# Second layer of an attention and two-layer expert kernel: how the seven Strassen products of a step are added up

## The chip, the cores and the metric

One core of a Trainium2 chip runs the whole kernel in one launch. The metric is device time in microseconds (us). Five engines work side by side, each through its own list of instructions in order: TensorE (PE; its weight loads have rows of their own, PEld), VectorE (DVE), ScalarE (ACT), GpSimd (POOL) and SyncE (SP), which here issues the DMAs. Matmul results land in PSUM, eight banks of 128 x 512 fp32; all else lives in SBUF.

## The reference, cut to what matters

Windowed attention gives a 2304 x 512 matrix x; a gated layer (512 to 1536 to 512) follows; then the second layer, which the change is about: eight experts, each a 512 to 1024 to 512 network with a ReLU, weighted by a router's probabilities.

```python
def _moe2_ref(x, w_gate, w1, w2):            # x (2304, 512), w1 (8, 512, 1024), w2 (8, 1024, 512)
    ...                                       # P: softmax of x @ w_gate, balanced 8 times by rows and columns
    out = np.zeros((N, D), dtype=np.float32)
    for e in range(E):
        h = np.maximum(x @ w1[e], 0.0)
        ye = h @ w2[e]
        out += P[:, e:e + 1] * ye
    return out.astype(np.float32)
```

## The kernel before, in words

**Precision.** Each fp32 operand is held as a high part rounded to fp32r and a low part (the rest). A product of two operands is three matmuls: high x high, high x low, low x high. `split` (L541 to L543) makes the parts: ACT casts the high one (L542), DVE subtracts to get the low one (L543).

**Steps.** The second layer runs over 96 steps (g, e, j): 3 groups of 768 tokens, 8 experts, 4 column pairs of w1. A step takes two 128-column blocks of w1 (j and j + 4) and computes hidden values for both, for both 384-token halves of the group. These four 128 x 384 results are one 2 x 2 block product, done with seven products in the Strassen-Winograd form, named M1 to M7. Each product is six matmuls of 128 x 384 (`emit_m`, L765, matmul L772): three passes by two halves of the depth. Passes one and two read the high weights, pass three the low ones, so the high weights of a product are last read by its 4th matmul. Products alternate between PSUM banks 6 and 7 (L767) in the order of `ORDER` (L763): M1, M6, M2, M7, M4, M5, M3.

**Adding up, before.** Each product is read out alone. ACT copies M1 (L785). DVE adds M6 to it (L787, u2), M2 to M1 (L789, the first result), M7 to u2 (L792, u3), subtracts M4 from u3 (L794, the third result), adds M5 to u3 (L797, the fourth result) and to u2 (L798), and M3 to u2 (L801, the second result). Each finished result goes through ReLU: ACT writes the high part (L805), DVE the low part (L806). A product's first weight load waits until the last reader of its bank's former content is done.

**Second matrix.** `emit_l2` (L810, matmul L818) multiplies the hidden values of the step before with w2: 36 matmuls of 128 x 512 into banks 0 to 5. In the program a step is its seven products, then the L818 matmuls of the step before, so the hidden values have a step's time to get ready. After four steps DVE adds each bank, weighted by P, to the output (L833).

**Weights.** The Strassen sums of w1 (`split_w1`, L604) are made on DVE (L610 once, then L609 three times, 128 x 256 each) in one scratch buffer, `o_sum`, and split into `o_wc[j]`. Four casts (and four L543) serve a step: A11 with A12 (used by M1 and M2), A22 (M4), S1 with S2 (M5 and M6), S3 with S4 (M7 and M3). They are written into the buffer that the running step still reads, so each cast waits for the 4th matmul of the last product that reads that piece, and the next sums wait until the scratch is read. w2 is split into `o_w2`. Both come by 256 KB DMAs (L501) into a ring of six slots; a DMA is issued when the slot's former content has been split. The x operands are split once per group (`split_x`, L621).

**Order.** The list `ev` gives the program's order, but the framework's scheduler sets the order on each engine; once set, an engine runs its list strictly in order. The router's column sums (`emit_cols`, L741) use eight columns of bank 7 and are put between products by `hooks` (L1013 to L1015).

Of the kernel before, what the change touches and what calls it, by code (L numbers as in the profile page):

```python
# [12 lines left out]
ALU = mybir.AluOpType  # L13
# [4 lines left out]
def attention_moe_moe2(  # L18
# [13 lines left out]
    nc = tc.nc  # L32
# [23 lines left out]
    HT = 128 * HTT  # L56
# [3 lines left out]
    for grp in groups:  # L60
        for half in grp:
            toks = [b * S + s + i for b, s, n in half for i in range(n)]
            for i in range(HTT):
                c = toks[i * 128:(i + 1) * 128]
# [89 lines left out]
    def area(name):  # L154
        if name not in areas:
            areas[name] = pool.tile([128, sizes[name]], F32R if name[-1] == "R" else F32, tag=name[0], name="area_" + name)
        return areas[name]

    PS = [psum.tile([128, 512], F32, name=f"ps{i}") for i in range(8)]

    def sl(o, n, r=False, p=slice(0, 128)):
        a = area(o.area)[p, o.off:o.off + n]
        if o.area[-1] == "R":
            return a if r else a.bitcast(F32)
        assert not r
        return a
# [319 lines left out]
    def load_w():  # L486
        n = w_load[0]
        if n >= len(raw_keys):
            return
        w_load[0] += 1  # L490
        key, i = raw_keys[n]
        src = sources(key)[i]
        if wide(key):
            dst = sl(o_wide[n % NWIDE], 1024).bitcast(I32)
        elif key[0] == "x":
            dst = sl(o_raw[n % NRAW], HT)
        else:
            dst = sl(o_raw[n % NRAW], 512)
        if len(src.shape) == 3:
            dst = dst.rearrange("p (k f) -> p k f", k=src.shape[1])  # L500
        nc.sync.dma_start(out=dst, in_=src)  # L501
# [39 lines left out]
    def split(src, hi, hi_f, lo):  # L541
        nc.scalar.copy(hi, src)  # L542
        nc.vector.tensor_tensor(out=lo, in0=src, in1=hi_f, op=ALU.subtract)  # L543

    def raw_slots(key):
        cnt = sum(1 for r in raw_keys if r[0] == key)
        n = w_next[0]
        assert raw_keys[n][0] == key
        w_next[0] += cnt
        return [o_raw[(n + i) % NRAW] for i in range(cnt)]  # L550
# [70 lines left out]
    def split_x(key):  # L621
        kk = key[2]
        b11, b12, b21, b22 = (sl(o, HT) for o in raw_slots(key))
        t = sl(o_sum, 4 * HT)
        t1, t2, t3, t4 = (t[:, HT * i:HT * i + HT] for i in range(4))
        sub = lambda o, a, b: nc.vector.tensor_tensor(out=o, in0=a, in1=b, op=ALU.subtract)
        sub(t1, b12, b11)
        sub(t2, b22, t1)
        sub(t3, b22, b12)
        sub(t4, t2, b21)  # L630
        view = lambda r: sl(o_xc, 28 * HT, r).rearrange("p (h m k n) -> p h m k n", h=2, m=7, n=HT)
        xr, xf = view(True), view(False)
        for src, m in ((b11, 0), (t2, 4), (b21, 1), (t3, 5), (t1, 3), (t4, 6), (b22, 2)):
            split(src, xr[:, 0, m, kk, :], xf[:, 0, m, kk, :], xr[:, 1, m, kk, :])
        for _ in range(4):
            load_w()
# [123 lines left out]

    steps = [(g, e, j) for g in range(NS) for e in range(NE) for j in range(NF2 // 2)]

    ORDER = (1, 6, 2, 7, 4, 5, 3)  # L763

    def emit_m(s, m):  # L765
        g, e, j = steps[s]
        ps = PS[6 + (7 * s + ORDER.index(m)) % 2][:, 0:HT]  # L767
        o = o_wc[j]
        i = 0
        for wp, xp in ((0, 0), (0, 1), (1, 0)):  # L770
            for kk in range(2):
                nc.tensor.matmul(  # L772
                    ps,
                    lhsT=sl(o + wp * (WC // 2) + A_OF[m] * 256 + kk * 128, 128, True),
                    rhs=sl(o_xc + xp * 14 * HT + (B_OF[m] * 2 + kk) * HT, HT, True),
                    start=(i == 0),
                    stop=(i == 5),
                )
                i += 1
        t = o_tmp[s % 2]  # L780
        m1, u2, u3, c21 = (sl(t + i * HT, HT) for i in range(4))
        h = o_h[s % 2]
        c = None
        if m == 1:
            nc.scalar.copy(m1, ps)  # L785
        elif m == 6:
            nc.vector.tensor_tensor(out=u2, in0=m1, in1=ps, op=ALU.add)  # L787
        elif m == 2:
            nc.vector.tensor_tensor(out=m1, in0=m1, in1=ps, op=ALU.add)  # L789
            c, i = m1, 0  # L790
        elif m == 7:
            nc.vector.tensor_tensor(out=u3, in0=u2, in1=ps, op=ALU.add)  # L792
        elif m == 4:
            nc.vector.tensor_tensor(out=c21, in0=u3, in1=ps, op=ALU.subtract)  # L794
            c, i = c21, 2
        elif m == 5:
            nc.vector.tensor_tensor(out=u3, in0=u3, in1=ps, op=ALU.add)  # L797
            nc.vector.tensor_tensor(out=u2, in0=u2, in1=ps, op=ALU.add)  # L798
            c, i = u3, 3
        else:  # L800
            nc.vector.tensor_tensor(out=u2, in0=u2, in1=ps, op=ALU.add)  # L801
            c, i = u2, 1
        if c is not None:
            hi, lo = h[2 * i], h[2 * i + 1]
            nc.scalar.activation(sl(hi, HT, True), c, AF.Relu)  # L805
            nc.vector.scalar_tensor_tensor(  # L806
                out=sl(lo, HT, True), in0=c, scalar=0.0, in1=sl(hi, HT), op0=ALU.max, op1=ALU.subtract
            )
# [71 lines left out]
    first = min(att)  # L880
# [130 lines left out]

    late = [("w1", 0, 0, 2), ("w2", 0, 0, 6), ("w1", 0, 0, 3), ("w2", 0, 0, 7)]
    hooks = {1: [("lg", NB - 1, 5)], 3: [("lgt", NB - 1, 5), ("gmax1",)], 5: [("gmax2", 5)]}  # L1013
    for it in range(8):
        hooks[13 + 2 * it] = [("cols", it, 7)]  # L1015
    pos = 0
    add("o", *prev)
    n_steps = len(steps)
# [1 line left out]
    for s in range(n_steps + 1):  # L1020
        for i, m in enumerate(ORDER):
            if s < n_steps:
# [43 lines left out]
    def banks(x):  # L1066
# [39 lines left out]
        "gmax2": lambda bk: emit_gmax2(banks(bk)),  # L1106
        "cols": lambda it, bk: emit_cols(it, banks(bk)),
        "m": emit_m,
        "l2": emit_l2,
    }  # L1110
# [32 lines left out]
```

## Time and profile before

| | |
|---|---|
| time, three runs | 2051.5, 2055.56, 2055.93 us (median 2055.56) |
| the profiled execution | span 2053.0 us from first to last instruction, between the fastest and the median run; the profile gives no other time for it |
| PE busy | 2040.6 us (99%) |
| PEld busy | 1803.5 us (88%) |
| DVE busy | 1473.4 us (72%) |
| ACT busy | 904.1 us (44%) |
| second layer, L772 and L818 | from 550.7 us to the end |

Busy time says how long an engine had an instruction in it. Where PE is busy all the time, what other engines do matters only if PE has to wait for it, and such a wait shows as idle time of PEld with the engine that ended it.

### The profile page before, as it was taken

Reading aid. Unit: us, or ns where it says so; the run is one execution under the profiler, and the core shown is the slowest. Engines: PE = TensorE matmul, PEld = TensorE weight load, DVE = VectorE, ACT = ScalarE, POOL = GpSimd, SP = SyncE. Lnnn points to the kernel's source line nnn. Section 1 sums busy time; section 2 is a strip of 40 time slices with the busy share of each in tenths; the row PEclk is TensorE's granted clock in tenths of the full one; section 3 lists DMA queues with packets and bytes.
Section 4 is the critical chain, followed back from the end, with each engine's and each line's share of the span. In section 5 each row is a group of like instructions: output and inputs, shape, how many; then the busy total and the mean of one; then the engine's idle time right before and its main releaser. Section 6 shows DMA issues by size and latency. Waiting matters only on the chain.

```text
span 2053.0 us, 30730 instructions
## 1 busy us (share of the span) xinstructions
PE 2040.6 (99%) x11189; PEld 1803.5 (88%) x11189; DVE 1473.4 (72%) x2987; ACT 904.1 (44%) x1800; POOL 42.5 (2%) x77
## 2 busy tenths in 40 slices
PE   8999999999999999999999999999999999999999
PEld 6887888888989899899989999989989999999997
DVE  7985555556897777767787677777688777677763
ACT  7756555655634334333343333333444333333331
POOL 3100000000000000000000000000000000000000
PEclk9999999999999999999999999999999999999999
DMA  9984453335622222222242222212224222222200
GB/s 250 271 265 119 109 139 103 109 91 165 186 78 72 62 72 73 62 64 76 63 128 72 73 62 72 72 62 65 75 63 128 75 70 62 72 72 62 69 25 31
DMA packets 235736, 197.05 MB, mean 96 GB/s; under 512 B 66880, under 2 KB 182080, under 8 KB 235584
## 3 DMA queue, kind: packets, MB, share of 16 engines
q1 hardware_dynamic: 235584, 195.10, 33.0%
q8 instruction: 87, 1.43, 0.3%
q14 instruction: 65, 0.53, 0.1%
HBM read 176.18 MB, written 18.87 MB: 95 GB/s over the span
## 4 chain that ended last, share of the span: by engine, by line
PE 96%; DVE 2%; ACT 1%; DMA 0%; issue 0%; DVEq 0%; ACTq 0%
PE ps L818 38%; PE ps L772 34%; PE ps L651 13%; PE ps L669 7%; PE ps L434 1%; PE ps L417 1%; PE ps L297 1%; PE ps L274 0%; DVE area_F L522 0%; DVE area_F L529 0%; PE ps L360 0%; PE ps L689 0%; ACT area_aF L515 0%; DVE area_bF L400 0%; DMA area_F<-saved 0%
## 5 line engine op out<-in xcount | busy, mean ns | idle before, releaser
L818 PE MATMUL ps<-area_aR,area_R 128*128 128x512 f32 x3456 | 808.1, 390 | 0.0
L818 PEld LDWEIGHTS ps<-area_aR,area_R 128*128 128x128 f32 x3456 | 646.7, 188 | 129.4
L772 PE MATMUL ps<-area_bR,area_R 128*128 128x384 f32 x4032 | 725.1, 336 | 0.0
L772 PEld LDWEIGHTS ps<-area_bR,area_R 128*128 128x128 f32 x4032 | 706.1, 188 | 11.3 <-DVE area_F L787 0.8
L542 ACT CAST area_R<-area_F 128x512 fp32r<-128x512 f32 (+1 forms) x528 | 302.2, 578 | 303.7 <-PE ps L772 168.2
L543 DVE TENSOR_TENSOR area_R<-area_F,area_R 128x512 fp32r<-128x512 f32 (+1 forms) x528 | 329.0, 638 | 89.9 <-ACT area_R L542 51.2
L542 ACT CAST area_aR<-area_F 128x512 fp32r<-128x512 f32 x192 | 119.3, 621 | 484.0 <-PE ps L818 470.1
L651 PE MATMUL ps<-area_R 128*128 128x512 f32 (+1 forms) x1440 | 313.6, 372 | 4.7 <-ACT area_F L656 3.3
L543 DVE TENSOR_TENSOR area_aR<-area_F,area_aR 128x512 fp32r<-128x512 f32 x192 | 131.6, 690 | 239.5 <-ACT area_aR L542 239.5
L651 PEld LDWEIGHTS ps<-area_R 128*128 128x128 f32 x1440 | 251.9, 190 | 54.5 <-ACT area_F L656 3.9
L805 ACT ACTIVATE area_R<-area_F 128x384 fp32r<-128x384 f32 x384 | 202.2, 527 | 191.8 <-DVE area_F L801 79.8
L806 DVE SCALAR_TENSOR_TENSOR area_R<-area_F,area_R 128x384 fp32r<-128x384 f32 x384 | 212.1, 552 | 2.0 <-ACT area_R L805 2.0
L669 PE MATMUL ps<-area_R 128*128 128x512 f32 (+1 forms) x720 | 162.6, 374 | 0.3 <-ACT area_R L660 0.3
L669 PEld LDWEIGHTS ps<-area_R 128*128 128x128 f32 x720 | 123.6, 189 | 24.2 <-issue 1.5
L609 DVE TENSOR_TENSOR area_F<-area_F 128x256 f32<-128x256 f32 x288 | 113.7, 421 | 2.4 <-DMA area_F<-in_moe_w_dram 0.3
L787 DVE TENSOR_TENSOR area_F<-area_F,ps 128x384 f32<-128x384 f32 x96 | 53.1, 553 | 73.4 <-PE ps L772 73.4
L833 DVE SCALAR_TENSOR_TENSOR area_F<-ps,area_F 128x512 f32<-128x512 f32 x126 | 94.3, 748 | 13.1 <-PE ps L818 12.6
L658 DVE TENSOR_TENSOR area_F<-area_F,ps 128x512 f32<-128x512 f32 (+1 forms) x60 | 37.9, 632 | 58.4 <-PE ps L651 50.1
L789 DVE TENSOR_TENSOR area_F<-area_F,ps 128x384 f32<-128x384 f32 x96 | 53.2, 554 | 35.6 <-PE ps L772 35.3
L785 ACT COPY area_F<-ps 128x384 f32<-128x384 f32 x96 | 46.0, 479 | 57.7 <-PE ps L772 57.2
L797 DVE TENSOR_TENSOR area_F<-area_F,ps 128x384 f32<-128x384 f32 x96 | 53.1, 553 | 14.4 <-PE ps L772 3.0
L792 DVE TENSOR_TENSOR area_F<-area_F,ps 128x384 f32<-128x384 f32 x96 | 52.7, 549 | 2.9 <-PE ps L772 2.9
(106 smaller groups left out, 1012.2 us busy)
## 6 DMA issues: line engine op xcount, KB each, us to landing
area_F<-in_moe_w_dram SPq DMA_DIRECT2D x384, 256.0 KB, 3.0
area_F<-saved SPq DMA_DIRECT2D x144, 256.0 KB, 2.8
saved<-area_F SPq DMA_DIRECT2D x18, 512.0 KB, 6.8
area_aF<-in_moe_w_gate_dram SPq DMA_DIRECT2D x12, 512.0 KB, 5.9
area_aF<-in_moe_w_val_dram SPq DMA_DIRECT2D x12, 512.0 KB, 6.2
area_aF<-in_moe_w_out_dram SPq DMA_DIRECT2D x12, 512.0 KB, 6.3
area_F<-x2d SPq DMA_DIRECT2D x24, 192.0 KB, 2.4
area_bF<-in_k_dram SPq DMA_DIRECT2D x16, 256.0 KB, 4.9
```

Source lines behind the costliest of these rows:

```text
L542: nc.scalar.copy(hi, src)
L543: nc.vector.tensor_tensor(out=lo, in0=src, in1=hi_f, op=ALU.subtract)
L609: sub = lambda o, a, b: nc.vector.tensor_tensor(out=o, in0=a, in1=b, op=ALU.subtract)
L651: nc.tensor.matmul(ps, lhsT=w3[:, kk, :], rhs=x3[:, kk, :], start=(i == 0), stop=(i == 3 * KD - 1))
L669: nc.tensor.matmul(PS[m][:, 0:n], lhsT=sl(o + 512 * wp + m * 128, 128, True), rhs=sl(oh + 512 * xp, n, True), start=(f == 0 and i == 0), s ...
L772: nc.tensor.matmul(ps, lhsT=sl(o + wp * (WC // 2) + A_OF[m] * 256 + kk * 128, 128, True), rhs=sl(o_xc + xp * 14 * HT + (B_OF[m] * 2 + kk) ...
L787: nc.vector.tensor_tensor(out=u2, in0=m1, in1=ps, op=ALU.add)
L789: nc.vector.tensor_tensor(out=m1, in0=m1, in1=ps, op=ALU.add)
L805: nc.scalar.activation(sl(hi, HT, True), c, AF.Relu)
L806: nc.vector.scalar_tensor_tensor(out=sl(lo, HT, True), in0=c, scalar=0.0, in1=sl(hi, HT), op0=ALU.max, op1=ALU.subtract)
L818: nc.tensor.matmul(PS[i], lhsT=sl(h[2 * q_ + hp] + c0, 128, True), rhs=sl(o + 512 * wp, 512, True), start=(j == 0 and fi == 0 and n == 0), ...
L833: nc.vector.scalar_tensor_tensor(out=a, in0=PS[i], scalar=p, in1=a, op0=ALU.mult, op1=ALU.add)
```

## The change

In the second layer TensorE adds up products itself. One chain runs in bank 6: M1, then M6, M7 and M4 each accumulate on what stands there; a second chain runs in bank 7: M5, then M3. M2 uses bank 7 alone, before M5. Between the products of a chain an engine reads the partial sum. The order is M1, M2, M6, M5, M7, M3, M4. The x operand of M4 changes its sign (L630), so that M4 can be added. ACT now copies three partial sums (M1, M1+M6, M5), DVE does three additions (r1 += M2, r3 += M1+M6+M7, r2 += M5+M3), and the third result is read by the ReLU directly from bank 6. The router's column sums move to places where no chain is open in bank 7.

```diff
-        sub(t4, t2, b21)
+        sub(t4, b21, t2)
...
-    ORDER = (1, 6, 2, 7, 4, 5, 3)
+    ORDER = (1, 2, 6, 5, 7, 3, 4)
+    CHAIN_A, CHAIN_B = (1, 6, 7, 4), (5, 3)
...
-        ps = PS[6 + (7 * s + ORDER.index(m)) % 2][:, 0:HT]
+        ps = PS[6 if m in CHAIN_A else 7][:, 0:HT]
+        first = m in (1, 2, 5)
+        last = m in (4, 2, 3)
...
-                    start=(i == 0),
+                    start=(first and i == 0),
                     stop=(i == 5),
+                    skip_group_check=not first,
...
+        add_ = lambda o: nc.vector.tensor_tensor(out=o, in0=o, in1=ps, op=ALU.add)
         if m == 1:
-            nc.scalar.copy(m1, ps)
+            nc.scalar.copy(r1, ps)
         elif m == 6:
-            nc.vector.tensor_tensor(out=u2, in0=m1, in1=ps, op=ALU.add)
+            nc.scalar.copy(r2, ps)
+        elif m == 5:
+            nc.scalar.copy(r3, ps)
         elif m == 2:
-            nc.vector.tensor_tensor(out=m1, in0=m1, in1=ps, op=ALU.add)
-            c, i = m1, 0
+            add_(r1)
+            c, q_ = r1, 0
         elif m == 7:
-            nc.vector.tensor_tensor(out=u3, in0=u2, in1=ps, op=ALU.add)
-        elif m == 4:
-            nc.vector.tensor_tensor(out=c21, in0=u3, in1=ps, op=ALU.subtract)
-            c, i = c21, 2
-        elif m == 5:
-            nc.vector.tensor_tensor(out=u3, in0=u3, in1=ps, op=ALU.add)
-            nc.vector.tensor_tensor(out=u2, in0=u2, in1=ps, op=ALU.add)
-            c, i = u3, 3
+            add_(r3)
+            c, q_ = r3, 3
+        elif m == 3:
+            add_(r2)
+            c, q_ = r2, 1
         else:
-            nc.vector.tensor_tensor(out=u2, in0=u2, in1=ps, op=ALU.add)
-            c, i = u2, 1
+            c, q_ = ps, 2
...
-    for it in range(8):
-        hooks[13 + 2 * it] = [("cols", it, 7)]
+    for it, at_ in enumerate((12, 14, 16, 19, 21, 23, 26, 28)):
+        hooks[at_] = [("cols", it, 7)]
```

In the changed file the line numbers shift: the matmul of a product is L775, the DVE addition L787, the ACT copies L789 (M1), L791 (M1+M6) and L793 (M5), the ReLU L807 and L808. In the rows below ps_71 is bank 6 and ps_72 bank 7.

On DVE, one step in the middle of the second layer, before (L787 reads M6, L789 M2, L792 M7, L794 M4, L797 and L798 M5, L801 M3):

```order
L787 TENSOR_TENSOR area_F<-area_F,ps_71 128x384
L789 TENSOR_TENSOR area_F<-area_F,ps_72 128x384
L543 TENSOR_TENSOR area_R<-area_F,area_R 128x512
L792 TENSOR_TENSOR area_F<-area_F,ps_71 128x384
L806 SCALAR_TENSOR_TENSOR area_R<-area_F,area_R 128x384
L794 TENSOR_TENSOR area_F<-area_F,ps_72 128x384
L543 TENSOR_TENSOR area_R<-area_F,area_R 128x256
L797 TENSOR_TENSOR area_F<-area_F,ps_71 128x384
L806 SCALAR_TENSOR_TENSOR area_R<-area_F,area_R 128x384
L798 TENSOR_TENSOR area_F<-area_F,ps_71 128x384
L806 SCALAR_TENSOR_TENSOR area_R<-area_F,area_R 128x384
L801 TENSOR_TENSOR area_F<-area_F,ps_72 128x384
```

The same stretch now (the three L787 read M2, then M1+M6+M7, then M5+M3):

```order
L787 TENSOR_TENSOR area_F<-area_F,ps_72 128x384
L543 TENSOR_TENSOR area_R<-area_F,area_R 128x512
L808 SCALAR_TENSOR_TENSOR area_R<-area_F,area_R 128x384
L543 TENSOR_TENSOR area_R<-area_F,area_R 128x512
L610 TENSOR_TENSOR area_F<-area_F 128x256
L787 TENSOR_TENSOR area_F<-area_F,ps_71 128x384
L609 TENSOR_TENSOR area_F<-area_F 128x256
L787 TENSOR_TENSOR area_F<-area_F,ps_72 128x384
L543 TENSOR_TENSOR area_R<-area_F,area_R 128x512
L808 SCALAR_TENSOR_TENSOR area_R<-area_F,area_R 128x384 x2
L808 SCALAR_TENSOR_TENSOR area_R<-ps_71,area_R 128x384
L543 TENSOR_TENSOR area_R<-area_F,area_R 128x256
```

The weight sums of the next w1 block (L610, L609), which stood behind all the additions, have moved in between them; the second L543 (the low part of S1 and S2) and L610 stand right ahead of the addition that reads bank 6 after M7. These three stand so in 81 of the 96 steps.

On ACT, the same step before (L785 copies M1, L805 is the ReLU, L542 the casts: A11 with A12, then A22, then S1 with S2, then S3 with S4):

```order
L785 COPY area_F<-ps_72 128x384
L542 CAST area_R<-area_F 128x512
L805 ACTIVATE area_R<-area_F 128x384
L542 CAST area_R<-area_F 128x256
L805 ACTIVATE area_R<-area_F 128x384
L542 CAST area_R<-area_F 128x512
L805 ACTIVATE area_R<-area_F 128x384
L542 CAST area_R<-area_F 128x512
L805 ACTIVATE area_R<-area_F 128x384
```

And now:

```order
L789 COPY area_F<-ps_71 128x384
L542 CAST area_R<-area_F 128x512
L807 ACTIVATE area_R<-area_F 128x384
L791 COPY area_F<-ps_71 128x384
L542 CAST area_R<-area_F 128x512
L793 COPY area_F<-ps_72 128x384
L542 CAST area_R<-area_F 128x512
L807 ACTIVATE area_R<-area_F 128x384
L542 CAST area_R<-area_F 128x256
L807 ACTIVATE area_R<-area_F 128x384
L807 ACTIVATE area_R<-ps_71 128x384
```

The second cast (S1 with S2) now stands between the copies of M1+M6 and of M5. TensorE's order keeps its shape: in all but the first steps and those around the two group changes it is 42 product matmuls by sixes on alternating banks, then 36 of the second matrix.

## Rows read from the trace of the kernel before

**Rows 1.** The page's head and its busy times by engine.
```profile
span 2053.0 us, 30730 instructions
PE 2040.6 (99%) x11189; PEld 1803.5 (88%) x11189; DVE 1473.4 (72%) x2987; ACT 904.1 (44%) x1800; POOL 42.5 (2%) x77
```
**Rows 2.** The chain that ended last, by engine.
```profile
PE 96%; DVE 2%; ACT 1%; DMA 0%; issue 0%; DVEq 0%; ACTq 0%
```
**Rows 3.** Groups by line: names, shapes, count, then busy us, mean ns, then idle before.
```profile
L772 PEld LDWEIGHTS ps<-area_bR,area_R 128*128 128x128 f32 x4032 | 706.1, 188 | 11.3 <-DVE area_F L787 0.8 <-ACT area_F L785 0.5 <-ACT area_R L542 0.4
...
L787 DVE TENSOR_TENSOR area_F<-area_F,ps 128x384 f32<-128x384 f32 x96 | 53.1, 553 | 73.4 <-PE ps L772 73.4
```
**Rows 4.** Timeline of PE over one step: start us, duration us, engine, line, count.
```profile
1201.24 7.49 PE L772 MATMUL ps<-area_bR,area_R 128*128 128x384 f32 x42
1208.58 8.36 PE L818 MATMUL ps<-area_aR,area_R 128*128 128x512 f32 x36
1216.78 0.51 PE L772 MATMUL ps<-area_bR,area_R 128*128 128x384 f32 x2
```
**Rows 5.** Timeline of all engines in the same step, ACT and DVE rows.
```profile
1201.42 1.37 DVE L543 TENSOR_TENSOR area_aR<-area_F,area_aR 128x512 fp32r<-128x512 f32 x2 [3.65 <-ACT area_aR L542]
1202.56 0.48 ACT L785 COPY area_F<-ps 128x384 f32<-128x384 f32 x1 [0.50 <-PE ps L772]
1203.62 0.55 DVE L787 TENSOR_TENSOR area_F<-area_F,ps 128x384 f32<-128x384 f32 x1 [0.83 <-PE ps L772]
1204.24 0.62 ACT L542 CAST area_R<-area_F 128x512 fp32r<-128x512 f32 x1 [1.20 <-PE ps L772]
1204.59 0.56 DVE L789 TENSOR_TENSOR area_F<-area_F,ps 128x384 f32<-128x384 f32 x1 [0.42 <-PE ps L772]
1205.06 0.69 DVE L543 TENSOR_TENSOR area_R<-area_F,area_R 128x512 fp32r<-128x512 f32 x1
1205.18 0.53 ACT L805 ACTIVATE area_R<-area_F 128x384 fp32r<-128x384 f32 x1 [0.32 <-DVE area_F L789]
1205.66 0.55 DVE L792 TENSOR_TENSOR area_F<-area_F,ps 128x384 f32<-128x384 f32 x1
...
1211.74 0.42 DVE L610 TENSOR_TENSOR area_F<-area_F 128x256 f32<-128x256 f32 x1
```
**Rows 6.** Timelines of single instructions, short windows in that step.
```profile
1200.76 0.62 ACT L542 CAST area_aR<-area_F 128x512 fp32r<-128x512 f32 x1 [5.52 <-PE ps L818]
1203.87 0.51 PE L772 MATMUL ps<-area_bR,area_R 128*128 128x384 f32 x2
1204.22 0.19 PEld L772 LDWEIGHTS ps<-area_bR,area_R 128*128 128x128 f32 x1
1212.08 0.76 DVE L609 TENSOR_TENSOR area_F<-area_F 128x256 f32<-128x256 f32 x2
1212.87 0.42 DVE L609 TENSOR_TENSOR area_F<-area_F 128x256 f32<-128x256 f32 x1
```
**Rows 7.** Timeline around a late weight load, and the PE rows of its step.
```profile
936.81 7.79 PE L772 MATMUL ps<-area_bR,area_R 128*128 128x384 f32 x42
939.53 0.55 DVE L787 TENSOR_TENSOR area_F<-area_F,ps 128x384 f32<-128x384 f32 x1 [0.60 <-PE ps L772]
940.14 0.64 PEld L772 LDWEIGHTS ps<-area_bR,area_R 128*128 128x128 f32 x4 [0.34 <-DVE area_F L787]
952.64 4.55 PE L772 MATMUL ps<-area_bR,area_R 128*128 128x384 f32 x25
```
**Rows 8.** One w1 DMA of that step, and landing times of L501, 640 to 1990 us.
```profile
1202.82 0.38 SPq L501 DMA_DIRECT2D area_F<-in_moe_w_dram  x1
DMA to landing us min/median/max: 3.2/3.2/3.2
DMA to landing us min/median/max: 2.3/2.9/5.0
```

More of the change, by code (lines that the diff above doesn't have):

```diff
@@ L780, in emit_m @@
         t = o_tmp[s % 2]
-        m1, u2, u3, c21 = (sl(t + i * HT, HT) for i in range(4))
+        r1, r2, r3 = (sl(t + i * HT, HT) for i in range(3))
         h = o_h[s % 2]
-        c = None
+        add_ = lambda o: nc.vector.tensor_tensor(out=o, in0=o, in1=ps, op=ALU.add)
         if m == 1:
-            nc.scalar.copy(m1, ps)
+            nc.scalar.copy(r1, ps)
         elif m == 6:
-            nc.vector.tensor_tensor(out=u2, in0=m1, in1=ps, op=ALU.add)
+            nc.scalar.copy(r2, ps)
+        elif m == 5:
+            nc.scalar.copy(r3, ps)
         elif m == 2:
-            nc.vector.tensor_tensor(out=m1, in0=m1, in1=ps, op=ALU.add)
-            c, i = m1, 0
+            add_(r1)
+            c, q_ = r1, 0
         elif m == 7:
-            nc.vector.tensor_tensor(out=u3, in0=u2, in1=ps, op=ALU.add)
-        elif m == 4:
-            nc.vector.tensor_tensor(out=c21, in0=u3, in1=ps, op=ALU.subtract)
-            c, i = c21, 2
-        elif m == 5:
-            nc.vector.tensor_tensor(out=u3, in0=u3, in1=ps, op=ALU.add)
-            nc.vector.tensor_tensor(out=u2, in0=u2, in1=ps, op=ALU.add)
-            c, i = u3, 3
-        else:
-            nc.vector.tensor_tensor(out=u2, in0=u2, in1=ps, op=ALU.add)
-            c, i = u2, 1
-        if c is not None:
-            hi, lo = h[2 * i], h[2 * i + 1]
+            add_(r3)
[3 more added lines that the diff above has]
+            c, q_ = r2, 1
+        else:
+            c, q_ = ps, 2
+        if last or m == 7:
+            hi, lo = h[2 * q_], h[2 * q_ + 1]
             nc.scalar.activation(sl(hi, HT, True), c, AF.Relu)
```

## The prediction, made before the changed kernel ran

> **What bounds the kernel now.** I read the busy times first: PE is busy 99% of the 2053.0 us span, PEld 88%, DVE 72%, ACT 44% [rows 1]. The chain that ended last runs on PE for 96% of its length [rows 2]. So DVE work that is taken away is not time gained; it counts only where PE waits for DVE. The groups by line say how much that is: the 4032 weight loads of the products stand idle 11.3 us in all, of which 1.7 us is put down to DVE and ACT by name [rows 3]. That is the ceiling of any gain in the products. The PE timeline of one step shows the rest: 42 product matmuls in 1208.58 - 1201.24 = 7.34 us, so 0.175 us each and 1.05 us a product, then 36 matmuls of the second matrix, and the next step begins at 1216.78, 15.54 us after this one [rows 4]. PE has no holes to fill. The question is whether the change opens some.
>
> **How close the waits run.** Products alternate between two banks. The first weight load of a product waits for the last reader of the product two places ahead. In the step shown, L787 (the reader of M6) ends at 1203.62 + 0.55 = 1204.17, and the weight load of M7, which waits for it, starts at 1204.22, 0.05 us later [rows 5, 6]. A weight load starts about one matmul (0.17 us) before its own matmul, so before the change M7 gets its bank with nothing to spare. A late case stands in the trace too: at 940.14 a weight load comes after 0.34 us of idle, released by an L787 that ended at 939.53 + 0.55 = 940.08; that step took 952.64 - 936.81 = 15.83 us, 0.29 us more than the usual 15.54 [rows 4, 7]. So a late release is paid almost in full, about the idle less 0.05 us.
>
> **The change part by part.**
>
> Four DVE additions fewer per step: 96 x 4 x 0.553 us = 212 us of DVE time [rows 3], by itself worth nothing, since PE does not wait for it. Two more ACT copies per step: 96 x 2 x 0.48 = 92 us of ACT [rows 5], also beside PE as such. The number and shape of matmuls stay. What a sum into an occupied place in PSUM costs against a first write can be read from the products as they are: five of the six matmuls of each already add, at the same pitch; I take nothing. The sign of t4 costs nothing. The column sums move by one or two products in the first five steps; PE waits for their DVE work before too, with little idle; I take nothing, with 1 us either way.
>
> The waits of one step, with the order of the changed kernel. Let t be the time since its first product.
> - M6 (3rd) waits for the copy of M1: it starts 1202.56 - 1201.24 = 1.32 and lasts 0.48, so it ends at 1.80 [rows 4, 5]. M6's weight load is due at 2 x 1.05 - 0.17 = 1.93. Covered.
> - M5 (4th) waits for r1 += M2. M2 is the second product, as M6 was, so this is the wait on L787 of before, with the same 0.05 us. No change.
> - M7 (5th) waits for the copy of M1+M6. The ReLU of r1 stands ahead of it: r1 ends at 1204.17 - 1201.24 = 2.93, the ReLU follows by 0.03 (1205.18 after L789's end at 1205.15) and lasts 0.53, to 3.49 [rows 5]. M6's result is there at about 3.4, so the copy ends at about 3.5 + 0.48 = 3.97 at most, and the weight load is due at 4 x 1.05 - 0.17 = 4.03. Covered, by less than 0.1 us.
> - M3 (6th) waits for the copy of M5, which now stands behind the cast of S1 and S2. That cast cannot start before the 4th matmul of M5 is done. Before, the 4th matmul of M2 starts at 1203.87 and the cast that waits for it at 1204.24: 0.37 later [rows 5, 6]. M5 starts at 3.15, its 4th matmul 3 x 0.173 = 0.52 later, the cast at 3.15 + 0.52 + 0.37 = 4.04, for 0.62, and the copy ends at 4.66 + 0.48 = 5.14 or a little earlier; due 5 x 1.05 - 0.17 = 5.08. Late by up to 0.06, which costs about 0.03.
> - M4 (7th) waits for r3 += M1+M6+M7, and here is the loss. Ahead of that addition on DVE stand the low part of S1 and S2 (L543), which needs the cast just named, and L610, which overwrites the scratch that L543 reads. Counted from the start of M5: 4th matmul 0.52; cast 0.37 after it, lasting 0.62; L543 0.04 after the cast (1201.42 against 1200.76 + 0.62), lasting 0.69; L610 0.03 after that, if it waits for L543's end as the third L609 waits for the second (1212.87 against 1212.08 + 0.76), lasting 0.42 [rows 5, 6]; the addition, which may start 0.09 before the end of an instruction it does not depend on (1205.66 against 1205.06 + 0.69 = 1205.75), lasting 0.55; the weight load 0.05 later. The sum is 0.52 + 0.37 + 0.62 + 0.04 + 0.69 + 0.03 + 0.42 - 0.09 + 0.55 + 0.05 = 3.20 us. The weight load of M4 is due three products after the start of M5, less a matmul: 3 x 1.05 - 0.17 = 2.98. It comes 0.22 us late. If M3 was late by a little, that much is paid already and the total is the same, since the path starts at M5.
>
> The cost of 0.22 us late: the row of the late load gives 0.29 for 0.34 of idle, so 0.18 us is what I take per step. Before, the additions stood ahead of the sums of w1, and L610 ran at 1211.74, when no product waited [rows 5]; that cover is gone. M1 of the next step waits for the last reader of M4, which has the 8.2 us of the second matrix as cover. At the end of the kernel the second matrix of the step before the last covers the same reader.
>
> Bounds of this term: if L610 need not wait for L543's end (0.12 us less) the load is 0.10 late, 0.06 us a step; if the copy of M1+M6 is late by its last 0.1 us, nothing is added, since it still ends before the cast can start; if the cast or the sums are held by a DMA, more (rival 3). The three instructions stand so in 81 of 96 steps: 81 x 0.18 = 14.6 us; with 0.06, 4.9 us. In the other 15 steps (the first ones and those at the two group changes) the order is irregular both before and now. I take nothing for them; their price is bounded by the longest wait by name among the products, 0.34 us each [rows 7], so 5 us, or by a like gain of 2 us.
>
> **Sum.** 2053.0 + 14.6 = 2067.6 us for an execution like the profiled one. The median of the three runs is 2055.56, 2.6 us over that span, so 2070 us.
>
> **Rivals.**
> 1. *The chain is covered after all, no change.* If the releases came 0.2 us earlier than worked out, every product would start on time, and 2052 to 2057 us would come out. For it: PE waits next to nothing today. Against: each term of the 3.20 is a row, and 0.22 is more than the roundings of all of them.
> 2. *Faster.* Place: M7's wait on L787, the tight one of before. Price: 1.7 us by name, and at most the 11.3 us of idle of the product weight loads [rows 3]; half of it gone would be 2050. It decides if r1 += M2 came earlier than L787 did; but M2 stands where M6 stood, and the same copy goes before. So little speaks for it.
> 3. *L610 waits for its DMA.* L610 ran 10.5 us into the step and now is due at 3.15 + 2.27 = 5.4. Its w1 block is asked for at 1202.82, 1.58 into the step, and lands 3.2 later, at 4.8 [rows 5, 8]: 0.6 us of cover. The landing times reach 5.0, so that in some steps it would be 1 us late. If transfers were slowed by 1 us throughout, 0.4 us more per step: 81 x 0.4 = 32 us, 2102. The median of 2.9 speaks against it.
> 4. *Weights loaded further ahead.* A load that had been made before the wait would be late only against its matmul: 0.22 - 0.17 = 0.05 us a step, 4 us, 2060 us. Against it: in the late case the weight load itself sat idle and the step paid 0.29 of 0.34 [rows 7].
>
> The Trainium skill, page TensorE: Matmul & The Clock Gate, section Back-to-back issue gap, describes the spacing of a stream of load and matmul pairs as set by both and pipelined through a reorder window 64 deep. By that rule rival 4 would hold; this trace shows a load that starts one matmul ahead and waits.
>
> **How the numbers follow.** My forecast (a hole before M4, 0.06 to 0.25 us in most steps, 2060 to 2080) gets 0.74. Rival 1 gets 0.12, rival 2 0.04, rival 3 0.06, rival 4 0.04. What a measurement can tell from no change is about 0.2%, 4.1 us, so from 2051.5 to 2059.7. Faster: rival 2, 0.04. Same: rival 1 and half of rival 4 and of what lies at the lower edge of my own case, 0.15. Slower: 0.81. The range for 8 in 10 reaches down to rival 1's upper edge, 2056, and up to 2084: the forecast with 0.25 us a step (2076) and the irregular steps (5) and some late DMAs (3).
>
> **What would show it.** Right: in the profile after, weight loads of L775 idle for about 0.2 us some 80 times, put down to DVE L787, 14 to 18 us in all; steps of 15.7 us; the seventh product begins late, not the others; L610 starts right after L543 ends; DVE busy near 1261 us and ACT near 996. Wrong: steps of 15.54 us; or the idle named after ACT L793 (then the copy, not the sums, is the bound), after ACT L791, or L610 waiting for a DMA.

## The result, and the profile after

| | before | after |
|---|---|---|
| time, median | 2055.48 us (2051.5 to 2055.93, 4 runs) | 2078.53 us (2074.73 to 2080.06, 4 runs) |
| span of the profiled execution | 2053.0 us | 2077.1 us |

The ratio to the kernel before is 1.0114, 95% interval 1.0102 to 1.0126: slower, by 23 us. The forecast was 2070, range 2056 to 2084. The direction and the place of the loss were right; the size was not, because a second loss, in eight steps only, had been left out of the sum.

The head of the page, the busy times and the chain by engine, after; they answer to [rows 1, 2]:

```profile
span 2077.1 us, 30256 instructions
PE 2058.4 (99%) x11189; PEld 1799.0 (87%) x11189; DVE 1300.4 (63%) x2603; ACT 966.6 (47%) x1992; POOL 40.9 (2%) x77
PE 94%; DMA 2%; DVE 2%; ACT 1%; issue 0%; SPq 0%; DVEq 0%; ACTq 0%
```

DVE has 173 us less to do, and no time came of it. The chain gives DMA 2% where it stood at 0%: some transfers now stand on the chain that ended last. The groups by line (busy us, mean ns, then idle before and its releasers) answer to [rows 3]; the last row is L610 in the kernel before:

```profile
L775 PEld LDWEIGHTS ps<-area_bR,area_R 128*128 128x128 f32 x4032 | 701.0, 188 | 39.3 <-DVE area_F L787 27.4 <-ACT area_F L789 1.0 <-ACT area_F L793 0.5
...
L610 DVE TENSOR_TENSOR area_F<-area_F 128x256 f32<-128x256 f32 x96 | 40.7, 424 | 11.6 <-DMA area_F<-in_moe_w_dram 9.0
```
```profile
L610 DVE TENSOR_TENSOR area_F<-area_F 128x256 f32<-128x256 f32 x96 | 40.2, 419 | 1.5 <-DMA area_F<-in_moe_w_dram 1.5
```

The product weight loads stand idle 39.3 us, 28 more than before, and 27.4 of it is put down to the DVE additions. L610 now waits 9.0 us for transfers. The 1.5 us of before is one wait at 508 us, ahead of the second layer, and it is still there; in the second layer L610 waited for no transfer before. Two views of waits from 550 us on (total us, times, longest), of the weight loads and of DVE, give the counts:

```profile
PEld ps L775 <- DVE area_F L787: 27.4, 84, 1.6
```
```profile
DVE area_F L610 <- DMA area_F<-in_moe_w_dram: 7.5, 9, 1.4
```

84 waits with a longest of 1.6: not all are the 0.2 us that was forecast. So there are two kinds of step. First the usual one. The timelines of PE, ACT, DVE and PEld for the stretch that [rows 4 to 6] show of before:

```profile
1195.30 7.71 PE L775 MATMUL ps<-area_bR,area_R 128*128 128x384 f32 x42
1202.85 8.37 PE L820 MATMUL ps<-area_aR,area_R 128*128 128x512 f32 x36
1211.06 0.33 PE L775 MATMUL ps<-area_bR,area_R 128*128 128x384 f32 x1
```
```profile
1199.37 0.62 ACT L542 CAST area_R<-area_F 128x512 fp32r<-128x512 f32 x1 [0.18 <-PE ps L775]
1199.89 0.47 ACT L793 COPY area_F<-ps 128x384 f32<-128x384 f32 x1
```
```profile
1200.02 0.69 DVE L543 TENSOR_TENSOR area_R<-area_F,area_R 128x512 fp32r<-128x512 f32 x1 [0.64 <-ACT area_R L542]
1200.75 0.43 DVE L610 TENSOR_TENSOR area_F<-area_F 128x256 f32<-128x256 f32 x1
1201.09 0.55 DVE L787 TENSOR_TENSOR area_F<-area_F,ps 128x384 f32<-128x384 f32 x1
```
```profile
1201.69 0.82 PEld L775 LDWEIGHTS ps<-area_bR,area_R 128*128 128x128 f32 x5 [0.24 <-DVE area_F L787]
```

The step takes 1211.06 - 1195.30 = 15.76 us instead of 15.54, and the 36 matmuls of the second matrix still take their 8.2. Cast, low part, L610, addition, weight load follow one another as worked out: counted from the step's first product the cast starts at 4.07 (forecast 4.04), the weight load at 6.39 (forecast 3.15 + 3.20 = 6.35).

The other kind: a step whose w1 block landed late. Of its second w1 DMA, issued 1.57 us into the step, the view by line gives the landing time; behind it the rows of DVE, PEld and PE:

```profile
DMA to landing us min/median/max: 4.5/4.5/4.5
```
```profile
726.49 0.42 DVE L610 TENSOR_TENSOR area_F<-area_F 128x256 f32<-128x256 f32 x1 [0.81 <-DMA area_F<-in_moe_w_dram]
726.83 0.55 DVE L787 TENSOR_TENSOR area_F<-area_F,ps 128x384 f32<-128x384 f32 x1
727.43 0.64 PEld L775 LDWEIGHTS ps<-area_bR,area_R 128*128 128x128 f32 x4 [1.02 <-DVE area_F L787]
727.43 0.79 PE L775 MATMUL ps<-area_bR,area_R 128*128 128x384 f32 x3 [0.70 <-DVE area_F L787]
```

L610 waits 0.81 us for the transfer, the addition stands behind it in DVE's queue, and M4's first weight load comes 1.02 us late. The same DMA in the kernel before, then that step's L610 and the PE rows around it:

```profile
DMA to landing us min/median/max: 4.6/4.6/4.6
```
```profile
729.84 0.42 DVE L610 TENSOR_TENSOR area_F<-area_F 128x256 f32<-128x256 f32 x1
```
```profile
720.76 6.08 PE L772 MATMUL ps<-area_bR,area_R 128*128 128x384 f32 x34
726.68 8.36 PE L818 MATMUL ps<-area_aR,area_R 128*128 128x512 f32 x36
734.88 2.44 PE L772 MATMUL ps<-area_bR,area_R 128*128 128x384 f32 x13
```

It was late before too (4.6 us), and it cost nothing, since L610 ran at 10.5 us into the step and the block had landed at 6.2.

The whole difference, from the start times of all matmuls of the second layer (distance to the next start, less the usual 0.173 us of a 384-column and 0.227 us of a 512-column matmul):

| us | before | after |
|---|---|---|
| first product starts at | 550.80 | 549.94 |
| gaps over by less than 0.06 us, sum | 9.5 | 11.0 |
| over by 0.06 to 0.25 | 2.2 | 17.9 |
| over by more than 0.25 | 0.5 | 8.1 |

Of the 24.1 us that the span grew, 15.7 are the hole before M4 (15.3 of it stands at M4's first two matmuls), 7.6 are eight steps in which L610 waited for its transfer (gaps of 0.47 to 1.42 us, the usual 0.2 included), 1.5 small gaps; the earlier start gives back 0.9. The steps of irregular order came out 1.2 us longer in all, the 81 others 23.6.

### The profile page after: what moved, and what is told of

It reads as the page before. It is cut to its first block, busy times and chain, and to the rows that moved or that the text cites. A ratio compares the mean times of both kernels' runs of the same rounds, so it can differ in the third digit from the quotient of the medians.

```text
span 2077.1 us, 30256 instructions
## 1 busy us (share of the span) xinstructions
PE 2058.4 (99%) x11189; PEld 1799.0 (87%) x11189; DVE 1300.4 (63%) x2603; ACT 966.6 (47%) x1992; POOL 40.9 (2%) x77
## 4 chain that ended last, share of the span: by engine, by line
PE 94%; DMA 2%; DVE 2%; ACT 1%; issue 0%; SPq 0%; DVEq 0%; ACTq 0%
PE ps L820 38%; PE ps L775 33%; PE ps L651 13%; PE ps L669 7%; DMA area_F<-in_moe_w_dram 1%; PE ps L434 1%; PE ps L417 1%; PE ps L297 1%; PE ps L274 0%; DMA area_bF<-in_k_dram 0%; DMA saved<-area_F 0%; DVE area_F L529 0%; DVE area_F L522 0%; PE ps L360 0%; DVE area_F L787 0%
## 5 line engine op out<-in xcount | busy, mean ns | idle before, releaser
L775 PE MATMUL ps<-area_bR,area_R 128*128 128x384 f32 x4032 | 742.2, 339 | 6.6 <-DVE area_F L787 6.4
L775 PEld LDWEIGHTS ps<-area_bR,area_R 128*128 128x128 f32 x4032 | 701.0, 188 | 39.3 <-DVE area_F L787 27.4
L542 ACT CAST area_R<-area_F 128x512 fp32r<-128x512 f32 (+1 forms) x528 | 304.5, 581 | 269.8 <-PE ps L775 146.9
L543 DVE TENSOR_TENSOR area_R<-area_F,area_R 128x512 fp32r<-128x512 f32 (+1 forms) x528 | 335.8, 641 | 142.4 <-ACT area_R L542 102.3
L542 ACT CAST area_aR<-area_F 128x512 fp32r<-128x512 f32 x192 | 119.1, 621 | 608.7 <-PE ps L820 597.2
L543 DVE TENSOR_TENSOR area_aR<-area_F,area_aR 128x512 fp32r<-128x512 f32 x192 | 131.6, 691 | 374.4 <-ACT area_aR L542 374.4
L787 DVE TENSOR_TENSOR area_F<-area_F,ps 128x384 f32<-128x384 f32 x288 | 158.5, 550 | 86.9 <-PE ps L775 85.8
L807 ACT ACTIVATE area_R<-area_F 128x384 fp32r<-128x384 f32 x288 | 150.6, 524 | 54.7 <-DVE area_F L787 54.6
L808 DVE SCALAR_TENSOR_TENSOR area_R<-area_F,area_R 128x384 fp32r<-128x384 f32 x288 | 160.0, 556 | 7.9 <-ACT area_R L807 2.6
L669 PEld LDWEIGHTS ps<-area_R 128*128 128x128 f32 x720 | 123.6, 189 | 24.1 <-issue 1.5
L609 DVE TENSOR_TENSOR area_F<-area_F 128x256 f32<-128x256 f32 x288 | 114.6, 420 | 0.1
L789 ACT COPY area_F<-ps 128x384 f32<-128x384 f32 x96 | 46.0, 479 | 61.8 <-PE ps L775 61.7
L808 DVE SCALAR_TENSOR_TENSOR area_R<-ps,area_R 128x384 fp32r<-128x384 f32 x96 | 52.9, 551 | 0.0
L610 DVE TENSOR_TENSOR area_F<-area_F 128x256 f32<-128x256 f32 x96 | 40.7, 424 | 11.6 <-DMA area_F<-in_moe_w_dram 9.0
L660 ACT CAST area_R<-area_F 128x512 fp32r<-128x512 f32 (+1 forms) x60 | 34.7, 578 | 27.7 <-DVE area_F L658 27.6
```

Of the source, the lines that this page charges most:

```text
L669: nc.tensor.matmul(PS[m][:, 0:n], lhsT=sl(o + 512 * wp + m * 128, 128, True), rhs=sl(oh + 512 * xp, n, True), start=(f == 0 and i == 0), s ...
L775: nc.tensor.matmul(ps, lhsT=sl(o + wp * (WC // 2) + A_OF[m] * 256 + kk * 128, 128, True), rhs=sl(o_xc + xp * 14 * HT + (B_OF[m] * 2 + kk) ...
L787: add_ = lambda o: nc.vector.tensor_tensor(out=o, in0=o, in1=ps, op=ALU.add)
L789: nc.scalar.copy(r1, ps)
L808: nc.vector.scalar_tensor_tensor(out=sl(lo, HT, True), in0=c, scalar=0.0, in1=sl(hi, HT), op0=ALU.max, op1=ALU.subtract)
```

## The experiments

The theory (A): DVE's queue ahead of the r3 addition makes M4 late, by 0.2 us in the usual step and by more when L610's transfer is late. The chief rival (B): it costs TensorE itself something to go on adding into a bank that was read between. Ratios are to the kernel before, whose runs the kernels of one group shared: 2055.39 us median for the sums held back, the two more slots, the read in free order and the sums on GpSimd; 2055.05 for the read with tied order and the cover under M4.

**Sums held back.** The changed kernel, with L610 told to stand behind the last addition of its step, as before.

```diff
         nc.vector.tensor_tensor(out=s1, in0=a21, in1=a22, op=ALU.add)
+        t = (key[2] * NE + key[1]) * (NF2 // 2) + key[3]
+        if t - 5 in last_add:
+            tc.add_manual_dep(nc.cur_bb.bb.instructions[-1], last_add[t - 5].name, ...)
```

> The changed kernel with one thing more: the first sum of a w1 block (L610 in the changed kernel) is told to stand behind the last addition (r2 += M5+M3) of the step in which it runs, as it did before the change; all else is as changed. Theory A (the hole before M4 is the path cast of S1 and S2, L543, L610, addition; and eight long waits are L610 waiting for its DMA): r3 += M1+M6+M7 can start when M7 is done, about 5.5 us into the step, and its bank is free at 6.1, just when M4's weight load is due, so steps fall from 15.74 to 15.5 - 15.56 us, no long waits are left, and the time is 2053 to 2058 us. Theory B (accumulating in one bank with reads in between costs the hole by itself, whatever the order on DVE): the 0.2 us before M4 stay, only the long waits go, 2068 to 2073 us.

Measured: 2058.74 us (2056.86 to 2060.21), ratio 1.0017 (1.0008 to 1.0025). Its groups by line, PE over one step, and on DVE in the next step the addition that reads bank 6 after M7 and the first sum:

```profile
L785 PEld LDWEIGHTS ps<-area_bR,area_R 128*128 128x128 f32 x4032 | 708.0, 188 | 11.5 <-ACT area_F L799 0.9 <-DVE area_F L797 0.7 <-ACT area_F L803 0.5
```
```profile
1196.62 8.36 PE L831 MATMUL ps<-area_aR,area_R 128*128 128x512 f32 x36
1204.82 7.35 PE L785 MATMUL ps<-area_bR,area_R 128*128 128x384 f32 x41
```
```profile
1210.35 0.55 DVE L797 TENSOR_TENSOR area_F<-area_F,ps 128x384 f32<-128x384 f32 x1
...
1214.13 0.42 DVE L612 TENSOR_TENSOR area_F<-area_F 128x256 f32<-128x256 f32 x1
```

The addition starts 5.53 us into the step instead of 5.79, the first sum (L612 in this file) at 9.31. The chains are all there, with their reads between, and the loads are idle 11.5 us against 11.3 before. Some 20 of the 23 us are gone with the place of the sums, the holes of the late transfers among them. B, by which the 0.2 us would have stayed, falls. The time is 0.7 us above A's range: the first product starts at 552.08, 1.3 later than before, and small gaps are 2.6 more. The median step is 15.57, 0.03 over before.

**Two more slots.** The changed kernel with a ring of eight slots from the third step's w1 block on, so that w1 comes earlier (a scratch buffer is made smaller to fit it).

```diff
-    o_tmp = takes("F", 4 * HT, 2)
+    o_tmp = takes("F", 3 * HT, 2)
+    o_more = takes("F", 512, 2)
...
+        ring = [o_raw[(n0 + i) % NRAW] for i in range(NRAW)] + o_more
+        return ring[(n - n0) % 8]
```

> The changed kernel with a ring of eight slots instead of six for the w1 and w2 blocks from the third step's w1 block on, so that each DMA is issued two loads earlier (half a step); the order on DVE and ACT is as changed. Theory A: the 0.2 us hole before M4 stays in the 81 regular steps (steps of 15.73 us), and the eight steps with 0.5 to 1.4 us more go, since L610's block has landed long before: 7 to 8 us less than the changed kernel, 2069 to 2073 us. Theory C (these eight long waits are not the DMA's fault but that of the group changes or the output additions): they stay, 2076 to 2080 us.

Measured: 2074.22 us (2071.12 to 2074.66), ratio 1.0089 (1.0075 to 1.0103). Its waits of the weight loads:

```profile
PEld ps L790 <- DVE area_F L802: 19.5, 83, 0.2
```

The waits are as many as in the changed kernel, and the longest is now 0.2 instead of 1.6; no sum of w1 waits for a transfer in the second layer any more. The long holes were the transfers, the short ones are not. 19.5 / 83 = 0.235 us late each; the median step is 15.75. The gaps of over 0.25 us shrink from 8.1 to 1.25 us in all, but the first product starts 1.6 us later than in the changed kernel and the gaps under 0.25 us are 0.9 more, so that 4.3 us are gained and the time ends 1 us above the range expected.

**One read more, free order.** The changed kernel with an added DVE copy of 128 columns of bank 6 ahead of the r3 addition.

```diff
         elif m == 7:
+            nc.vector.tensor_copy(sl(o_lgs[5], 128), ps[:, 0:128])
             add_(r3)
```

> The changed kernel with one more DVE instruction in every step: a copy of 128 columns of bank 6 (about 0.27 us, 0.18 us after overlap) just ahead of the addition r3 += M1+M6+M7. Theory A: the bank comes free 0.18 us later, and since that release is already late, all of it is paid: steps of 15.92 us, 14 to 16 us more than the changed kernel, 2091 to 2096 us. If DVE's queue were not on the path there, the copy would vanish beside TensorE: 2077 to 2081 us.

Measured: 2073.27 us (2071.63 to 2074.7), ratio 1.0088 (1.0074 to 1.0102). A miss: it was to be some 15 us slower than the changed kernel and was 5 us faster. PE over one step shows why:

```profile
1195.65 6.49 PE L775 MATMUL ps<-area_bR,area_R 128*128 128x384 f32 x36
1201.98 0.40 PE L821 MATMUL ps<-area_aR,area_R 128*128 128x512 f32 x1
1202.30 1.33 PE L775 MATMUL ps<-area_bR,area_R 128*128 128x384 f32 x6
1203.47 8.14 PE L821 MATMUL ps<-area_aR,area_R 128*128 128x512 f32 x35
```

The scheduler, given one more instruction, put a matmul of the second matrix ahead of M4, so the longer wait found work under it. The test changed two things at once and said nothing on the price of a read; it did suggest the next but one.

**One read more, order tied.** The same, with the second matrix tied behind all products of its step, as in the changed kernel.

```diff
+                tc.add_manual_dep(nc.cur_bb.bb.instructions[-1], last_mm[0].name, ...)   # each matmul of the second matrix
```

> The changed kernel with one more VectorE copy per step (128 columns of the bank of M4, ahead of the r3 addition), as in e4_read, but with TensorE's order tied to that of the changed kernel: 42 product matmuls, then the 36 of the second matrix. The result is the same; the copy's output is used by nothing. Theory A (the hole before M4 is VectorE's queue: copy, activation, sum, addition, one behind the other): the added copy of about 0.2 us lies on that path in full, the hole grows from 0.20 to about 0.38 us in 80 steps, regular steps go from 15.74 to 15.9 us, 2090 to 2096 us in all. Rival B (what is late before M4 is the chain's read itself, whatever VectorE does ahead of it): hole and time as in the changed kernel, 2075 to 2081 us.

Measured: 2104.58 us (2103.65 to 2105.79), ratio 1.0242 (1.0225 to 1.0259). DVE and PEld in one step, then PE's first products of this step and the next:

```profile
1200.35 0.69 DVE L543 TENSOR_TENSOR area_R<-area_F,area_R 128x512 fp32r<-128x512 f32 x1 [0.63 <-ACT area_R L542]
1201.07 0.42 DVE L610 TENSOR_TENSOR area_F<-area_F 128x256 f32<-128x256 f32 x1
1201.42 0.28 DVE L799 COPY area_F<-ps 128x128 f32<-128x128 f32 x1
1201.62 1.08 DVE L788 TENSOR_TENSOR area_F<-area_F,ps 128x384 f32<-128x384 f32 x2
```
```profile
1202.21 0.82 PEld L775 LDWEIGHTS ps<-area_bR,area_R 128*128 128x128 f32 x5 [0.43 <-DVE area_F L788]
```
```profile
1195.64 7.91 PE L775 MATMUL ps<-area_bR,area_R 128*128 128x384 f32 x42
...
1211.59 1.23 PE L775 MATMUL ps<-area_bR,area_R 128*128 128x384 f32 x6
```

The copy takes 0.28 us and puts the addition 0.19 us later in the step (5.98 against 5.79); the load is 0.43 us late instead of 0.24, and the step takes 15.95 instead of 15.76. What stands ahead of the addition on DVE is paid one for one, in each step. The total is some 9 us above A's range, and that is not this price: over the whole layer the steps take 25.8 us more than in the changed kernel, 9.7 of it in the first four. That the tie took away cover which the second matrix had given there is likely, and was not tried by itself. The other 91 steps take 16.1 us more, 0.18 each.

**Sums on GpSimd.** The changed kernel, with L610 and L609 made by GpSimd instead of DVE.

```diff
-        sub = lambda o, a, b: nc.vector.tensor_tensor(out=o, in0=a, in1=b, op=ALU.subtract)
-        nc.vector.tensor_tensor(out=s1, in0=a21, in1=a22, op=ALU.add)
+        sub = lambda o, a, b: nc.gpsimd.tensor_tensor(out=o, in0=a, in1=b, op=ALU.subtract)
+        nc.gpsimd.tensor_tensor(out=s1, in0=a21, in1=a22, op=ALU.add)
```

> The changed kernel with the four sums of each w1 block (L610, L609) made by GpSimd instead of DVE. Theory A: nothing but L543 stands ahead of r3 += M1+M6+M7, so the hole before M4 goes as with the sums held back: 2053 to 2058 us, if GpSimd needs less than some 2.5 us for each sum (four of them have about 10 us). Theory B: 2068 to 2073 us. If GpSimd is slower than that, or slows DVE down while both work, casts come late and the time is above 2080 us.

Measured: 2072.67 us (2068.82 to 2073.6), ratio 1.0082 (1.0068 to 1.0095), between the two expectations. The sums by line on POOL, two late rows of PE, one ahead of the second layer and one at a group change, and a cast of the latter on ACT:

```profile
L609 POOL TENSOR_TENSOR area_F<-area_F 128x256 f32<-128x256 f32 x288 | 247.9, 872 | 181.3 <-DVE area_R L543 100.6 <-DMA area_F<-in_moe_w_dram 72.9
L610 POOL TENSOR_TENSOR area_F<-area_F 128x256 f32<-128x256 f32 x96 | 73.0, 761 | 1082.3 <-DVE area_R L543 870.0 <-PE ps L651 117.7 <-DMA area_F<-in_moe_w_dram 81.7
```
```profile
557.63 0.74 PE L669 MATMUL ps<-area_R 128*128 128x256 f32 x4 [3.36 <-ACT area_R L660]
```
```profile
1059.76 0.45 PE L775 MATMUL ps<-area_bR,area_R 128*128 128x384 f32 x1 [1.92 <-ACT area_F L789]
```
```profile
1056.53 0.62 ACT L542 CAST area_R<-area_F 128x512 fp32r<-128x512 f32 x1 [3.70 <-POOL area_F L609]
```

In the usual step the hole is gone (median 15.55 us), as A has it. But a sum takes 0.76 to 0.87 us there against 0.42 on DVE. Where sums are wanted at once, the casts wait for them on ACT and other work stands behind the casts: the first product starts at 558.2, 7.4 us later than before, and the steps of the two group changes take 19.3 and 19.2 us.

**Cover under M4.** The changed kernel, with the first six matmuls of the second matrix ahead of M4 in the program.

```diff
             if s < n_steps:
+                if m == 4 and s > 0:
+                    add("l2", s - 1, 0)
                 add("m", s, m)
...
-            if s > 0:
+            if s > 0 and (n > 0 or s == n_steps):
                 add("l2", s - 1, n)
```

> The changed kernel with the first six matmuls of the second matrix of the step before put ahead of M4 on TensorE (36 product matmuls, 6 of the second matrix, the 6 of M4, the other 30): M4's first weight load is due 1.36 us later, all work is the same. Theory A (VectorE's queue is 0.2 us late for M4, and in eight steps a late transfer of a weight block makes it up to 1.5 us late): the hole of 0.2 us goes in every step and nearly all of the eight long ones; two more changes per step between 384 and 512 columns may cost some 0.05 us; steps of 15.53 to 15.60 us, 2056 to 2063 us in all. Rival B (to read a bank and go on adding into it costs TensorE the time, wherever it stands): the hole stays before M4's matmuls, 2074 to 2081 us.

Measured: 2058.51 us (2056.02 to 2060.3), ratio 1.0016 (1.0006 to 1.0025). PE over one step, the group of the weight loads' waits on the addition, and DVE's wait for the transfers:

```profile
1195.87 1.21 PE L775 MATMUL ps<-area_bR,area_R 128*128 128x384 f32 x6
1196.91 7.00 PE L820 MATMUL ps<-area_aR,area_R 128*128 128x512 f32 x30
1203.75 6.46 PE L775 MATMUL ps<-area_bR,area_R 128*128 128x384 f32 x36
1210.05 1.55 PE L820 MATMUL ps<-area_aR,area_R 128*128 128x512 f32 x6
1211.44 1.21 PE L775 MATMUL ps<-area_bR,area_R 128*128 128x384 f32 x6
```
```profile
PEld ps L775 <- DVE area_F L787: 0.5, 2, 0.4
```
```profile
DVE area_F L610 <- DMA area_F<-in_moe_w_dram: 6.1, 7, 1.2
```

DVE's queue is as it was and L610 still waits 6.1 us for late transfers, yet PE waits 0.5 us where it waited 27.4. With 1.4 us of other matmuls ahead of M4 both losses are covered at once. B, by which the hole goes with the chain, falls a second time. The median step is 15.57 us, 0.04 over before. That this is the more frequent change between the two matmul widths fits the place of the small gaps that are new (1.2 us at M4, 1.8 at the second-matrix matmuls after it, in all steps together), but was not tried by itself.

No kernel tried beats the one before. Its gaps sum to 12 us over the whole second layer, so that little was there to win.

## Why the prediction was right, and where its size was off

1. *DVE work taken away is worth nothing.* Right: 173 us less on DVE, no time gained, in any kernel here.
2. *The hole before M4, 0.18 us in 81 steps, 14.6 us.* Right in mechanism, place and count: 84 waits, of which eight are long, and 15.7 us on PE without the long ones; with more slots, where the long ones are gone, 83 waits are left. Each piece of the 3.20 us path is in the trace. In the step shown the lateness was 0.24 instead of 0.22, and the median step paid 0.21 of it (15.74 against 15.53). The sums held back and the tied copy show the cause from both sides: take L610 out of the queue and the hole closes, put 0.19 us in and it grows by 0.2.
3. *M3's wait on the copy of M5, late by up to 0.06.* Not seen. The copy starts 0.10 before the cast ends (1199.89 against 1199.37 + 0.62 = 1199.99), an overlap that I had counted for DVE and not for ACT. M6, M5 and M7 are covered, as forecast.
4. *A sum into an occupied bank, with reads between, costs nothing.* Right to within 0.03 us a step, which is what the kernel with sums held back is over the one before. It is not the adding as such: of its gaps under 0.06 us the third and fifth products (M6 and M7, which add onto a bank just read) have 0.3 and 0.9 us in all 96 steps, the third and fifth of before 0.4 and 0.8. M4 has 2.1 us and M3 0.7 more than the products in their places before, but with the sums on GpSimd, where both add onto the same banks, M4 has only 0.1 more and M3 1.8. What these small gaps are stays open.
5. *Late transfers.* This is the step that failed. Rival 3 took the landing time as one number for all steps: either all are late, 2102, or none is, with 3 us for "some" in the range and none in the sum. "L610 waiting for a DMA" stood among the signs of being wrong, and it came, in eight long waits that cost 7.6 us. The trace of before had more to say. The 2.9 us median that spoke against the rival is that of all L501 transfers [rows 8]; the DMA that L610 waits for, the second of a w1 block, has 3.2. The one in the prediction was issued 1.58 us into the step, but of the 81 from the fifth step on, those around the group changes left out, 20 were issued at 2.15 or a little later and landed at 5.25 by the median, which leaves 0.2 us of cover and not 0.6. Issue time and landing time added, step by step, seven of the 81 landed after L610's new time of 5.42, by 3.7 us in all. So some 4 us were to be had from the trace of before; the rest is that more were late after (of 342 w1 and w2 DMAs between 640 and 1990 us, 3 of before and 7 of after took 4.4 us or more). Why more were is open.
6. *Rival 4, weights loaded further ahead.* By it a late release would cost 0.05 us a step. The step paid 0.20. The Trainium skill, page TensorE: Matmul & The Clock Gate, section Back-to-back issue gap, speaks of loads and matmuls pipelined through a reorder window 64 deep. In these traces a load that waits for a bank starts only when that wait is over. M4's first load starts 0.17 us ahead of its matmul where it is in time (median of before), together with it where it is late (0.00 after), and 0.43 us late costs 0.4 (15.95 against 15.54).
7. *Busy times.* DVE came out at 1300 instead of 1261 us, ACT at 967 instead of 996. I had subtracted whole durations. On DVE an instruction that does not depend on the one ahead, and waits for nothing, starts about 0.09 us before that one ends (1201.09 against 1200.75 + 0.43), so taking away 384 of 0.553 us frees 173 / 384 = 0.45 us each. ACT likewise: the durations grew by 88 us, the busy time by 63.

With 15.7 and 7.6 in place of 14.6 and 0 the sum would have been 2079 by the median. That 2078.5 lies in the range is owed in part to luck: its upper end holds 5 us for the irregular steps, which came to 1.2, and 3 us for late transfers, which came to 7.6.

## What to carry to other kernels

Where the bottleneck engine hardly ever waits, removing work elsewhere buys nothing, and the order of what is left is the whole risk: look at what the scheduler has moved ahead of the one instruction that the bottleneck waits for, and add up that queue. When an instruction that reads a transfer moves earlier, price it step by step, issue time plus landing time against the new cover, and for that transfer alone, not by the median of all. Here six independent matmuls ahead of the waiting one, or one ordering edge, undid nearly all of a loss for which the cheaper arithmetic had not made up.

## What the runs showed of the hardware that was not expected

The late transfers recur in the same places. The second w1 DMA of one step took 4.6 us in the trace of before and 4.5 in that of after, where 3.2 is the median of these DMAs. This is step 11 (the first being 0); in steps 52 and 75, too, it took over 4.4 us both before and after. The steps 11, 34 and 75 were long by it both in the changed kernel and in the one with a read more in free order. So it looks like a fixed meeting of transfers rather than chance; which ones meet was not tried.

A ReLU that reads its 128 x 384 from PSUM took ACT less time than one from SBUF: 0.475 us against 0.524, the means of 96 and 288 instructions after.
